# Unused matrix products tied to batch 0's transposed tiles, and another spacing of batch 1's Fourier steps

## The chip, the cores and the metric

The kernel runs on one core of one Trainium2 chip. The core has a matrix engine (TensorE, PE in the rows, with its weight loads as PEld), a vector engine (VectorE, DVE), a scalar engine (ScalarE, ACT), GpSimd (POOL) and a queue engine (SyncE, SP) that issues most transfers. The metric is the time of one execution in microseconds (us).

## The reference

For 8 batches of 576 positions, 8 heads of 64: attention with a window of 128 keys and a bias that falls with distance; the heads side by side are x (576 x 512). Then the real part of a Fourier transform over positions and features, added to x; a normalization per position; a two-layer net with ReLU, added again.

```python
attn = exp(scores - max) / (sum + 1e-09)        # |rel| bias, 0 <= rel < 128
x = (attn @ v).transpose(0, 2, 1, 3).reshape(B, S, 512)
u = x + real(fft(fft(x, axis=1), axis=2))
un = (u - mean(u)) / sqrt(var(u) + 1e-06)
out = u + relu(un @ w_ch1) @ w_ch2               # 512 -> 2048 -> 512
```

## The kernel before

Work is cut into batches and, in a batch, into four pairs of heads; p counts pairs over all batches (p = 4 b + j). One pair has three groups of scores (`scores`, L378); each group's result is reduced on DVE (L391, which also makes the row's minimum `nb`), put through the exponential on ACT and multiplied with v (`values`, into `pv`). Batches 0 and 1 (`NF = 2`) do this in fp32: the exponentials P are transposed on TensorE (`turn`, L422, into the PSUM tile `sp`), ACT copies them into an SBUF tile `pt` (L426, six buffers), and `values` multiplies `pt` with `vr` (L440). From batch 2 on all is split into fp16 high and low parts, and `pt` comes by a transposing DMA (L413).

After a batch's attention comes its Fourier transform (`fourier`): `fold_a` to `fold_d` (DVE, ACT), four `rows` (PE, L555), `middle`, three `cols` (PE, L589) with `cols_out` (ACT) and `cols_add` (DVE: `ds`, `X`, `ut`, L607 to L618), then `norm` (DVE, POOL, ACT `un`) and a transposing DMA into `uT`. Then the net (`ffn`): W1 products (L699) into `fp`, ACT's ReLU (L704) and DVE's remainder into `hbuf`, W2 products (L713) into `fp`. In the first 100 us the weights are read from DRAM as 64-bit words and put together by ACT (L183) and three DVE operations per chunk (L188 to L190), 32 chunks in all; four small products per chunk (`gram`, L198) find their scale.

The order of the work is set in two steps. Each piece is put into a queue with a due time (`put`, and `after`, which adds to the time of the piece at work); pieces are taken in order of due time, and this order is the priority with which a scheduler (with a model of the engines) then places every instruction in its engine's own order. On the chip each engine takes its instructions in just that order and waits where one isn't ready. `PACE`, `T1`, `DFT` and `START` set the due times of batches; in `fourier` the factor `f` spaces the transform's steps.

Some matrix products are computed and never read: `busy(p)` issues three of them (`SPIN`) after each `scores`, each `turn` and each `values` of batch 0's pairs (p < 4), of 128 x 512 columns, from the cosine table `tab1_sb` into a PSUM tile `spin`, an `fp` buffer. That is 15 calls for each of the four pairs, 180 products (L299).

Of the kernel before, what the change touches and what calls it, by code (L numbers as in the profile page):

```python
# [12 lines left out]
BF16 = mybir.dt.bfloat16  # L13
# [35 lines left out]
DFT = 24 + LC + 0.4  # L49
START = DFT + 17  # L50
PACE, T1 = (0.37, 0.5), 9.0
SPIN = 3
SLOW = 1.4


def begin_of(p):
    return 6 * PACE[0] * p if p < 4 else T1 + 6 * (p - 4)
# [19 lines left out]
def attn_fft_ffn_kernel(  # L77
# [16 lines left out]
    V, A, G, T = nc.vector, nc.scalar, nc.gpsimd, nc.tensor  # L94
# [14 lines left out]
    tab1_sb = const.tile([128, 4, 3, NS], F16, name="tab1_sb")  # L109
# [44 lines left out]
    def put(t, f, *a):  # L154
        heappush(queue, (t, next(order), f, a))

    def after(dt, f, *a, **kw):
        put(now[0] + dt, lambda: f(*a, **kw))  # L158
# [133 lines left out]

    raws, ops, Ps, pts, pvs, vmx = {}, {}, {}, {}, {}, {}
    spin = ps_f.tile([128, 512], F32, name="fp")
    trig = tab1_sb.rearrange("p a b c -> p (a b c)")

    def busy(p):
        for _ in range(SPIN if p < 4 else 0):
            T.matmul(spin, trig[:, 0:128], trig[:, 0:512], start=True, stop=True)  # L299

    def load(p):
        b, j = divmod(p, 4)
# [53 lines left out]
    def keys(t, ti):  # L356
        a0 = TILES[ti][2][0][1]
        if ti == 2:
            return view(t, 128, (65, 2), (1, 128))
        return t[:, a0:a0 + 128 * len(TILES[ti][2])]  # L360

    def scores(p, i):
        b, j = divmod(p, 4)
        if b < NF:
            prods = ((ops[p][0], ops[p][1]),)
        else:
            qh, ql, kh, kl = ops[p][:4]
            prods = ((qh, kh), (ql, kh), (qh, kl))
        grp = SGRP[i]
        sp = [ps_s.tile([128, 512], F32, name=f"sp{e}") for e in range(2)]  # L370
        col = 0
        for ti in grp:
            c0, m, blks = TILES[ti]
            n = 128 * len(blks)
            for x, (qq, kk) in enumerate(prods):
                for e in range(2):
                    h = slice(64 * e, 64 * e + 64)
                    T.matmul(sp[e][:m, col:col + n], qq[h, c0:c0 + m], keys(kk[h], ti),  # L378
                             start=(x == 0), stop=(x == len(prods) - 1))
            col += n  # L380
        busy(p)
        P = Ps[p, i] = {}
        for e in range(2):
            h = 2 * j + e
            nb = small.tile([128, 5], F32, name="nb", bufs=6)
            col = 0
            for ti in grp:
                m, n, pc = TILES[ti][1], 128 * len(TILES[ti][2]), PCOL[ti]
                pt = P[e, ti] = att.tile([128, 256], F32, name="P", bufs=PB)
                tab, mul = (rel_sb, -2.0 ** -(h + 1)) if b < NF else (scs[b][2], scs[b][1][:m, h:h + 1])  # L390
                V.tensor_tensor_reduce(pt[:m, 0:n], sp[e][:m, col:col + n], tab[:m, pc:pc + n],  # L391
                                       mul, 3.0e38, ALU.add, ALU.min, nb[:m, ti:ti + 1])
                after(0.25, A.activation, pt[:m, 0:n], pt[:m, 0:n], AF.Exp, bias=nb[:m, ti:ti + 1], scale=-1.0)
                if b >= NF:
                    after(0.45, halves, p, i, e, ti)
                col += n
# [18 lines left out]
    def turn(p, i, e):  # L415
        tp = ps_s.tile([128, 512], F32, name=f"sp{e}")
        P = Ps[p, i]
        col = 0
        for ti in TGRP[i]:
            m, blks = TILES[ti][1:]  # L420
            for x in range(len(blks)):
                T.transpose(tp[:, col:col + m], P[e, ti][:m, 128 * x:128 * x + 128], ident[:m, :m])  # L422
                col += m
        pt = pts[p, i, e] = att.tile([128, 448], F32, name="pt", bufs=6)
        busy(p)
        A.activation(pt[:, :col], tp[:, :col], AF.Copy)  # L426

    def values(p, i, e):
        b, j = divmod(p, 4)
        pt = pts.pop((p, i, e))  # L430
        if i == 0:
            pvs[p] = ps_v.tile([128, 512], F32, name="pv")[:, 0:325].rearrange("p (a b) -> p a b", a=5)
        pv, col = pvs[p], 0
        for ti in TGRP[i]:
            m, blks = TILES[ti][1:]
            n = len(blks)
            for x, (vc, _) in enumerate(blks):
                first, last = x == 0, x == n - 1
                if b < NF:
                    T.matmul(pv[:, ti], pt[:, col:col + 128], ops[p][2][:, e, vc], start=first, stop=last)  # L440
                    col += m
                    continue
                vh, vl = ops[p][4:]
                ph, pl = (pt[:, o:o + 128] for o in (POUT[ti] + x * m, POUT[ti] + (n + x) * m))
                T.matmul(pv[:, ti], ph, vh[:, e, vc], start=first, stop=False)  # L445
                T.matmul(pv[:, ti, 0:D], ph, vl[:, e, vc], start=False, stop=False)  # L446
                T.matmul(pv[:, ti], pl, vh[:, e, vc], start=False, stop=last)  # L447
        busy(p)
        if i == 2:
            after(0.2, weigh, p, e, pv)  # L450

# [42 lines left out]
    def fourier(b, t0):  # L494
# [122 lines left out]
                V.tensor_tensor(ut[p0:p0 + 32], X2[0:32], ds[0:32, 0:512], ALU.add)  # L617
                V.tensor_tensor(ut[p0 + 64:p0 + 96], X2[64:96], ds[64:96, 0:512], ALU.add)  # L618

        f = SLOW if b else PACE[1]  # L620
        put(t0, begin)
        for c, t in ((2, 0.0), (0, 0.8), (1, 1.5)):
            if c < 2:
# [99 lines left out]
    for p in range(4 * B):  # L723
        b, j = divmod(p, 4)
        t, f = begin_of(p), 1 if b else PACE[0]
        put(t - 7 * f if p else -3.2, load, p)
        if b < NF:
            put(t - 3.8 * f if p else -2, convert, p, 0)
            put(t - 1.2 * f, load_v, p)
            put(t + 4.2 * f, v_max, p)  # L730
        else:
            early = p < 4 * NF + 2
            put(t - (1.3 if early else 6.8), load_v, p)
            for what, x in enumerate((4.6, 3.6, -2 if early else 1.2)):
                put(t - x, convert, p, what)
        for i in range(3):
            put(t + 2 * i * f, scores, p, i)
            for e in range(2 if b < NF else 0):
                put(t + (2 * i + e + LB + 0.33) * f, turn, p, i, e)
        for x in range(6):  # L740
            put(t + (x + LC + 0.66) * f, values, p, x % 3, x // 3)
        if b < NF and j == 3:
            put(t + 5 * f, f32_scale, b)
# [5 lines left out]
    for b in range(B):  # L749
        t = begin_of(4 * b)  # L750
        if b >= NF:
            batch_scales(b, *((t - 16.4, 0.72) if b == NF else (t - 26, 1.2)))
        fourier(b, transform_of(b))
        n = 80 if b % 2 else 64
        t = forward_of(b)
        put(t, step, ffn(b), t, (24 if b else forward_of(1) - t) / n)
# [87 lines left out]
def program(q, k, v, moe_w_ch1, moe_w_ch2):  # L844
    import numpy as np
    import concourse.bacc as bacc

    B = q.shape[0]
    qa = np.ascontiguousarray(q.transpose(0, 1, 3, 2)[..., query_order()]).reshape(B, 4, 128, NQ)
    ka = np.concatenate([k, k[:, :, :NK - S]], axis=2).transpose(0, 1, 3, 2)  # L850
    ka = np.ascontiguousarray(ka).reshape(B, 4, 128, NK)
    idx = np.array([[min(s + p, S - 1) for s in VSTART] for p in range(128)])
    va = np.ascontiguousarray(v[:, :, idx])
    nf = min(B, NF)
    v0 = np.ones((nf, H, 128, 5, 65), np.float32)
    v0[..., 0:D] = va[:nf]
    w1 = np.ascontiguousarray(moe_w_ch1.reshape(4, 128, 16, 128).transpose(1, 2, 0, 3).reshape(128, -1))
    w2 = np.ascontiguousarray(moe_w_ch2.reshape(16, 128, DM).transpose(1, 0, 2).reshape(128, -1))
    w1, w2 = w1.view(np.int64), w2.view(np.int64)
    rel, slope, tab1, tab2 = tables()  # L860
    nc = bacc.Bacc("TRN2", target_bir_lowering=False, num_devices=1, dynamic_dma_scratch_size=1024)
    arrays, args = {}, []
    for name, a in (("q", qa), ("k", ka), ("v", va), ("v0", v0), ("w1", w1), ("w2", w2), ("rel", rel),
                    ("slope", slope), ("tab1", tab1), ("tab2", tab2)):
        arrays[name + "_dram"] = a
        args.append(nc.dram_tensor(name + "_dram", a.shape, mybir.dt.from_np(a.dtype), kind="ExternalInput").ap())
    rows = B * S
    args.append(nc.dram_tensor("out_dram", (rows, DM), F32, kind="ExternalOutput").ap())
    with tile.TileContext(nc, schedule_with_timeline_sim=True) as tc:
        attn_fft_ffn_kernel(tc, *args)  # L870
    return nc, arrays, B
```

## Time and profile before

| | us |
|---|---|
| median of 3 runs (lowest, highest) | 1116.77 (1116.02, 1118.63) |
| the profiled execution's own time | 1116.72 |
| its span, first to last instruction | 1114.9 |
| TensorE busy / VectorE busy / ScalarE busy | 1069.6 / 712.8 / 580.8 |
| mean granted TensorE clock | 0.972 of full speed |

[...] In a window's row, the number after x counts instructions.

### The profile page before, as it was taken

Reading aid. Unit: us, or ns where it says so; the run is one execution under the profiler, and the core shown is the slowest. Engines: PE = TensorE matmul, PEld = TensorE weight load, DVE = VectorE, ACT = ScalarE, POOL = GpSimd, SP = SyncE. Lnnn points to the kernel's source line nnn. Section 1 sums busy time; section 2 is a strip of 40 time slices with the busy share of each in tenths; the row PEclk is TensorE's granted clock in tenths of the full one; section 3 lists DMA queues with packets and bytes.
Section 4 is the critical chain, followed back from the end, with each engine's and each line's share of the span. In section 5 each row is a group of like instructions: output and inputs, shape, how many; then the busy total and the mean of one; then the engine's idle time right before and its main releaser. Section 6 shows DMA issues by size and latency. Waiting matters only on the chain.

```text
span 1114.9 us, 23952 instructions
## 1 busy us (share of the span) xinstructions
PE 1069.6 (96%) x9296; PEld 737.2 (66%) x9296; DVE 712.8 (64%) x2081; ACT 580.8 (52%) x1380; POOL 20.3 (2%) x59
## 2 busy tenths in 40 slices
PE   6999989879699999999999999999999999999998
PEld 4667768465374857767667677585758577767665
DVE  6988678815966667777868485869685655262111
ACT  5757889647863555446645464456635441151000
POOL 0000000000000000000000000000000000010000
PEclk9999859999899999999999999999999999999999
DMA  9941558656775235432642154344532240020000
GB/s 367 341 153 44 172 131 205 162 156 158 202 145 133 68 82 112 88 97 50 131 106 78 44 110 98 92 77 101 115 83 44 53 89 1 20 48 20 19 11 20
DMA packets 191507, 117.83 MB, mean 106 GB/s; under 512 B 154400, under 2 KB 164128, under 8 KB 191392
## 3 DMA queue, kind: packets, MB, share of 16 engines
q1 hardware_dynamic: 190816, 114.84, 40.8%
q8 instruction: 73, 1.20, 0.5%
q10 hardware_dynamic: 576, 1.45, 0.3%
q14 instruction: 42, 0.34, 0.1%
HBM read 70.63 MB, written 9.44 MB: 72 GB/s over the span
## 4 chain that ended last, share of the span: by engine, by line
PE 69%; DMA 7%; DVE 6%; ACT 3%; issue 1%; SPq 1%; ACTq 0%; DVEq 0%
PE fp L699 29%; PE fp L713 29%; PE sp L378 4%; PE pd L555 2%; DMA pt<-P 2%; DMA wall<-v_dram 2%; DMA wall<-q_dram 2%; ACT wall L257 1%; PE pd L589 1%; PE pv L445 1%; DMA wall<-k_dram 1%; PE pv L447 1%; PE pv L446 1%; DVE P L391 1%; DMA uT<-un 1%
## 5 line engine op out<-in xcount | busy, mean ns | idle before, releaser
L713 PE MATMUL fp<-wall,hbuf 128*128 128x512 f16 x1728 | 397.1, 383 | 2.4 <-DVE hbuf L158 2.3
L699 PEld LDWEIGHTS <-wall 128*128 128x128 f16 x3840 | 340.1, 99 | 61.3 <-issue 14.5
L699 PE MATMUL fp<-uT,wall 128*128 128x256 f16 x3072 | 364.8, 276 | 14.0 <-DVE hbuf L158 8.3
L713 PEld LDWEIGHTS <-hbuf 128*128 128x128 f16 x1728 | 163.2, 99 | 187.2 <-issue 11.5
L158 ACT ACTIVATE P<-P,nb 128x256 f32<-128x256 f32 x320 | 142.9, 479 | 124.6 <-DVE nb L391 124.5
L158 DVE SCALAR_TENSOR_TENSOR hbuf<-fp,hbuf 128x512 f16<-128x512 f32 x144 | 99.0, 688 | 130.4 <-ACT hbuf L704 130.0
L704 ACT ACTIVATE hbuf<-fp 128x512 f16<-128x512 f32 x144 | 85.1, 591 | 186.7 <-PE fp L699 186.5
L391 DVE CUSTOM_DVE_ANT_0 P<-sp,rg,nsl 128x256 f32<-128x256 f32 x240 | 97.3, 450 | 59.7 <-PE sp L378 51.9
L158 DVE SCALAR_TENSOR_TENSOR P<-P 128x256 f16<-128x256 f32 x240 | 88.6, 390 | 26.9 <-ACT P L404 25.6
L378 PE MATMUL sp<-kk,qq 64*128 64x256 f16 (+5 forms) x880 | 93.4, 294 | 11.5 <-DVE nb L391 5.9
L404 ACT ACTIVATE P<-P 128x256 f16<-128x256 f32 x240 | 86.0, 384 | 7.6 <-DMA pt<-P 7.0
L257 ACT ACTIVATE wall<-wall 128x512 f32<-128x512 f32 (+2 forms) x90 | 54.6, 606 | 49.5 <-DMA wall<-v_dram 19.2
L445 PE MATMUL pv<-vhs,pt 128*128 128x65 f16 x432 | 55.5, 195 | 4.6 <-DMA pt<-P 3.4
L446 PE MATMUL pv<-vl,pt 128*128 128x64 f16 x432 | 56.0, 193 | 0.0
L447 PE MATMUL pv<-vhs,pt 128*128 128x65 f16 x432 | 55.9, 194 | 0.0
L158 DVE SCALAR_TENSOR_TENSOR X<-fp,misc,X 128x512 f32<-128x512 f32 x32 | 23.8, 744 | 44.7 <-PE fp L713 44.7
L378 PEld LDWEIGHTS <-qq 64*128 64x128 f16 (+1 forms) x720 | 32.3, 100 | 28.5 <-issue 24.9
L445 PEld LDWEIGHTS <-pt 128*128 128x128 f16 x432 | 41.1, 98 | 15.0 <-issue 4.5
L299 PE MATMUL fp<-tab_sb 128*128 128x512 f16 x180 | 45.5, 379 | 1.1 <-DMA tab_sb<-tab_dram 1.1
L699 PE MATMUL fp<-wall,wall 128*128 128x128 f16 x768 | 45.4, 219 | 0.1
L446 PEld LDWEIGHTS <-pt 128*128 128x128 f16 x432 | 40.7, 99 | 7.0
L440 PE MATMUL pv<-vr,pt 128*128 128x65 f32 x288 | 41.3, 294 | 0.3 <-ACT pt L426 0.3
(146 smaller groups left out, 1200.4 us busy)
## 6 DMA issues: line engine op xcount, KB each, us to landing
qr<-q_dram SPq DMA_DIRECT2D x32, 304.0 KB, 3.1
hbuf<-w_dram SPq DMA_DIRECT2D x16, 512.0 KB, 7.2
out_dram<-X SPq DMA_DIRECT2D x32, 256.0 KB, 2.2
wall<-v_dram SPq DMA_DIRECT2D x30, 256.0 KB, 2.9
vr<-v_dram SPq DMA_DIRECT2D x24, 320.0 KB, 3.6
kr<-k_dram SPq DMA_DIRECT2D x24, 289.0 KB, 3.4
wall<-q_dram SPq DMA_DIRECT2D x24, 256.0 KB, 2.9
wall<-k_dram SPq DMA_DIRECT2D x24, 256.0 KB, 2.9
```

What stands on the lines that cost most here:

```text
L158: put(now[0] + dt, lambda: f(*a, **kw))
L257: A.activation(t, t, AF.Square, accum_out=box["mx"][:, i, c:c + 1])
L299: T.matmul(spin, trig[:, 0:128], trig[:, 0:512], start=True, stop=True)
L378: T.matmul(sp[e][:m, col:col + n], qq[h, c0:c0 + m], keys(kk[h], ti), start=(x == 0), stop=(x == len(prods) - 1))
L391: V.tensor_tensor_reduce(pt[:m, 0:n], sp[e][:m, col:col + n], tab[:m, pc:pc + n], mul, 3.0e38, ALU.add, ALU.min, nb[:m, ti:ti + 1])
L404: A.activation(hi, P32, AF.Copy, scale=2.0 ** 14)
L445: T.matmul(pv[:, ti], ph, vh[:, e, vc], start=first, stop=False)
L446: T.matmul(pv[:, ti, 0:D], ph, vl[:, e, vc], start=False, stop=False)
L447: T.matmul(pv[:, ti], pl, vh[:, e, vc], start=False, stop=last)
L699: T.matmul(fp[:, i * n:(i + 1) * n], w1_ap(e, c, f0 + i), uT[:, j, c, 0:n], start=(c == 0 and p == 0), stop=(c == 3 and p == 2))
L704: A.activation(ht[:, 0], fp, AF.Relu)
L713: T.matmul(op, hh[f][:, a, i * 128:(i + 1) * 128], w2_ap(e, f), start=(f == 0 and p == 0), stop=(f == 15 and p == 2))
```

## The change

`busy` and its calls go. `idle_turns(pt)` takes their place: after the copy of a transposed tile into `pt`, for the pairs of batch 0 alone, six products of 128 x 256 columns are queued with a due time 1.2 later than the piece at work. They read the upper halves of the words of that `pt` (as bfloat16) and write the same unused PSUM tile. There are six such copies per pair and four pairs: 144 products. In `fourier`, `f` is 0.9 for batch 1 where it was `SLOW` = 1.4; batch 0 keeps 0.5 and the later ones 1.4.

```diff
--- before.py
+++ after.py
@@ -49,7 +49,7 @@
 DFT = 24 + LC + 0.4
 START = DFT + 17
 PACE, T1 = (0.37, 0.5), 9.0
-SPIN = 3
+SPIN, GAP = 6, 1.2
 SLOW = 1.4
 
 
@@ -292,11 +292,11 @@
 
     raws, ops, Ps, pts, pvs, vmx = {}, {}, {}, {}, {}, {}
     spin = ps_f.tile([128, 512], F32, name="fp")
-    trig = tab1_sb.rearrange("p a b c -> p (a b c)")
-
-    def busy(p):
-        for _ in range(SPIN if p < 4 else 0):
-            T.matmul(spin, trig[:, 0:128], trig[:, 0:512], start=True, stop=True)
+
+    def idle_turns(pt):
+        upper = pt[:, 0:256].bitcast(BF16).rearrange("p (x e) -> p x e", e=2)[:, :, 1]
+        for _ in range(SPIN):
+            T.matmul(spin[:, 0:256], upper[:, 0:128], upper, start=True, stop=True)
 
     def load(p):
         b, j = divmod(p, 4)
@@ -378,7 +378,6 @@
                     T.matmul(sp[e][:m, col:col + n], qq[h, c0:c0 + m], keys(kk[h], ti),
                              start=(x == 0), stop=(x == len(prods) - 1))
             col += n
-        busy(p)
         P = Ps[p, i] = {}
         for e in range(2):
             h = 2 * j + e
@@ -422,8 +421,9 @@
                 T.transpose(tp[:, col:col + m], P[e, ti][:m, 128 * x:128 * x + 128], ident[:m, :m])
                 col += m
         pt = pts[p, i, e] = att.tile([128, 448], F32, name="pt", bufs=6)
-        busy(p)
         A.activation(pt[:, :col], tp[:, :col], AF.Copy)
+        if p < 4:
+            after(GAP, idle_turns, pt)
 
     def values(p, i, e):
         b, j = divmod(p, 4)
@@ -445,7 +445,6 @@
                 T.matmul(pv[:, ti], ph, vh[:, e, vc], start=first, stop=False)
                 T.matmul(pv[:, ti, 0:D], ph, vl[:, e, vc], start=False, stop=False)
                 T.matmul(pv[:, ti], pl, vh[:, e, vc], start=False, stop=last)
-        busy(p)
         if i == 2:
             after(0.2, weigh, p, e, pv)
 
@@ -617,7 +616,7 @@
                 V.tensor_tensor(ut[p0:p0 + 32], X2[0:32], ds[0:32, 0:512], ALU.add)
                 V.tensor_tensor(ut[p0 + 64:p0 + 96], X2[64:96], ds[64:96, 0:512], ALU.add)
 
-        f = SLOW if b else PACE[1]
+        f = (SLOW if b > 1 else 0.9) if b else PACE[1]
         put(t0, begin)
         for c, t in ((2, 0.0), (0, 0.8), (1, 1.5)):
             if c < 2:
```

The first place is TensorE's order at the start of the program (before; `tab_sb` is the cosine table, `wall` the weights under assembly, L422 the transposes):

```order
L378 MATMUL sp_162<-kk,qq 96x256
L378 MATMUL sp_163<-kk,qq 96x256
L299 LDWEIGHTS tab_sb
L299 MATMUL fp<-tab_sb 128x512
...
L198 LDWEIGHTS wall_105
L198 MATMUL fp<-wall_105 128x128
...
L422 MATMUL sp_183<-ident,P 128x128 x3
L422 MATMUL sp_205<-ident,P 128x128 x3
L378 MATMUL sp_218<-kk,qq 128x256
L378 MATMUL sp_219<-kk,qq 128x256
L299 LDWEIGHTS tab_sb
```

The same place now (line numbers from here on are one less for `turn`, L421):

```order
L378 MATMUL sp_159<-kk,qq 96x256
L378 MATMUL sp_160<-kk,qq 96x256
L198 LDWEIGHTS wall_105
L198 MATMUL fp<-wall_105 128x128
...
L421 MATMUL sp_177<-ident,P 128x128 x3
L421 MATMUL sp_196<-ident,P 128x128 x3
L378 MATMUL sp_206<-kk,qq 128x256
L378 MATMUL sp_207<-kk,qq 128x256
L421 MATMUL sp_220<-ident,P 128x96 x2
L421 MATMUL sp_220<-ident,P 128x128 x2
L299 LDWEIGHTS pt
L299 MATMUL fp<-pt 128x256
```

Twelve products stood between the first scores and the first `gram`; now none stands there, and the first six come after the third group of transposes, with `pt` as their operand.

The second place is VectorE's order at the end of batch 1's transform (before; `ds`, `X`, `ut` are its last `cols_add`, `st` and `ag` its norm, L391 the reductions of scores):

```order
L391 ISA P,nb<-sp_3554,rg,nsl 96x256
L391 ISA nb 96x1
L607 TENSOR_TENSOR ds<-ab 33x257
...
L614 TENSOR_TENSOR X<-X,ds 1x512
L617 TENSOR_TENSOR ut<-X,ds 32x512
L618 TENSOR_TENSOR ut<-X,ds 32x512
L158 TENSOR_TENSOR un<-un 128x512
L661 BN_STATS st<-X 128x6 x2
L158 SCALAR_TENSOR_TENSOR X<-fp,misc,X 128x512
...
L391 ISA P,nb<-sp_3661,rg,nsl 128x256
```

The same place now (`r<-pd` begins the scales of batch 3, without which its scores can't start):

```order
L390 ISA P,nb<-sp_3330,rg,nsl 128x256
L390 ISA nb 128x1
L665 SCALAR_TENSOR_TENSOR nmr<-ag,rstd 128x2
L606 TENSOR_TENSOR ds<-ab 33x257
...
L613 TENSOR_TENSOR X<-X,ds 1x512
L616 TENSOR_TENSOR ut<-X,ds 32x512
L158 SCALAR_TENSOR_TENSOR X<-fp,misc,X 128x512
L617 TENSOR_TENSOR ut<-X,ds 32x512
...
L660 BN_STATS st<-X 128x6 x2
L147 TENSOR_SCALAR r<-pd 128x3
```

The last `cols_add` of batch 1 was rows 632 to 638 of VectorE's order and is now rows 586 to 594; the `r` of batch 3 is row 597 before and row 598 now, so the transform's end has moved from behind it to ahead of it.

## Rows read from the trace of the kernel before

**Rows 1.** The page: span, busy times, TensorE clock in tenths over 40 slices.

```profile
span 1114.9 us, 23952 instructions
PE 1069.6 (96%) x9296; PEld 737.2 (66%) x9296; DVE 712.8 (64%) x2081; ACT 580.8 (52%) x1380; POOL 20.3 (2%) x59
...
PEclk9999859999899999999999999999999999999999
```

**Rows 2.** Windows, per stretch: length, busy us and (x count) per engine, clock, DMA.

```profile
core 0: us, PE busy (x) PEld busy (x) DVE busy (x) ACT busy (x) POOL busy (x), PEclk, DMA share, GB/s
10.00:110.00 100.00, 96.82 (x675) 64.55 (x676) 90.49 (x268) 71.12 (x145) 0.11 (x1) 1.00 0.63 221
350.00:1115.00 765.00, 759.81 (x6984) 522.78 (x6982) 462.13 (x1313) 329.60 (x770) 14.32 (x33) 1.00 0.31 69
```

**Rows 3.** Windows of three stretches of the startup, columns as in Rows 2.

```profile
10.00:30.00 20.00, 17.98 (x112) 10.65 (x112) 18.69 (x55) 15.42 (x35) 0.00 (x0) 1.00 1.03 402
30.00:60.00 30.00, 30.00 (x200) 18.70 (x197) 29.97 (x87) 22.30 (x45) 0.00 (x0) 1.00 0.88 308
60.00:110.00 50.00, 48.84 (x369) 35.19 (x369) 41.83 (x129) 33.41 (x66) 0.11 (x1) 1.00 0.31 97
```

**Rows 4.** Page, part 5: the unused products, and the 256-column products of fp16.

```profile
L699 PE MATMUL fp<-uT,wall 128*128 128x256 f16 x3072 | 364.8, 276 | 14.0 <-DVE hbuf L158 8.3
...
L299 PE MATMUL fp<-tab_sb 128*128 128x512 f16 x180 | 45.5, 379 | 1.1 <-DMA tab_sb<-tab_dram 1.1
```

**Rows 5.** Waits of DVE, 60 to 110 us: total us, times, longest.

```profile
DVE ri L459 <- PE pv L440: 2.7, 1, 2.7
DVE wall L219 <- ACT wall L216: 2.5, 4, 1.3
DVE P L391 <- PE sp L378: 1.6, 2, 1.1
```

**Rows 6.** Waits of PE, 100 to 345 us, same columns.

```profile
PE sp L378 <- DVE nb L391: 5.4, 3, 4.9
...
PE pv L440 <- ACT pt L426: 0.3, 1, 0.3
```

**Rows 7.** Windows around the change of level at 138 us, columns as in Rows 2.

```profile
132.00:138.00 6.00, 5.59 (x47) 4.14 (x44) 4.10 (x17) 5.95 (x20) 0.20 (x2) 1.00 0.59 188
138.00:166.00 28.00, 24.19 (x96) 18.34 (x97) 20.24 (x84) 23.23 (x52) 1.56 (x4) 0.51 0.48 128
```

**Rows 8.** Timeline of PE: products of values (L440), and the first of rows (L555).

```profile
79.88 2.12 PE L440 MATMUL pv<-vr,pt 128*128 128x65 f32 x18
...
109.24 0.30 PE L555 MATMUL fp<-tab_sb,fh 128*128 128x289 f16 x1 [0.86 <-ACT fh L538]
...
153.04 4.10 PE L440 MATMUL pv<-vr,pt 128*128 128x65 f32 x18
```

**Rows 9.** Timeline of DVE near 295 us: start, us, operation.

```profile
293.46 0.08 DVE L391 DVE_READ_ACCUMULATOR2_ANT nb<- 96x1 f32 x1
296.45 0.68 DVE L618 TENSOR_TENSOR ut<-X,ds 32x512 f32<-32x512 f32 x1
```

**Rows 10.** Windows of 10 us later on, columns as in Rows 2.

```profile
230.00:240.00 10.00, 8.47 (x72) 7.01 (x72) 2.44 (x4) 5.43 (x16) 0.00 (x0) 0.83 0.55 147
290.00:300.00 10.00, 6.12 (x66) 3.28 (x64) 9.63 (x24) 10.00 (x23) 0.00 (x0) 0.96 0.54 153
300.00:310.00 10.00, 7.05 (x41) 4.99 (x41) 8.00 (x28) 7.18 (x18) 1.77 (x2) 0.53 1.05 244
```

**Rows 11.** Timeline of PE: three runs of W1 products after 230 us.

```profile
231.53 4.16 PE L699 MATMUL fp<-uT,wall 128*128 128x256 f16 x24 [3.31 <-DVE hbuf L158]
...
305.04 7.56 PE L699 MATMUL fp<-uT,wall 128*128 128x256 f16 x48 [1.38 <-DMA uT<-un]
...
321.73 5.41 PE L699 MATMUL fp<-uT,wall 128*128 128x256 f16 x48
```


## The prediction

> **What bounds the kernel now.** I read the page first: TensorE is busy for 96% of the span at a clock of 9 tenths or more in most slices, VectorE and ScalarE for about half to two thirds [rows 1]. A share over the whole span hides stages, so the windows came next. From 350 us to the end TensorE is busy for 759.8 of 765 us at the full clock; from 10 to 110 us it is nearly so too, but there VectorE is busy for 90.5 of the 100 us [rows 2]. Then I cut the startup into three: from 10 to 30 us the DMA engines are full, from 30 to 60 us both TensorE (30.00 of 30) and VectorE (29.97) are, from 60 to 110 us TensorE alone is (48.84 of 50; VectorE 41.83, DMA share 0.31) [rows 3]. Between 110 and 350 us TensorE waits here and there and runs at the lower clock in stretches.
>
> So a microsecond taken from TensorE counts fully only after 350 us, where the change takes nothing: apart from names and numbers TensorE's order there is the one it was. It counts in part from 60 to 110 us, and hardly before that. Whatever the program gains by 350 us it keeps to the end, since TensorE has hardly any idle time left in which to lose it.
>
> **The change part by part.**
>
> *The unused products.* Before, 180 products take 45.5 us of busy TensorE, 45.5 / 180 = 253 ns each [rows 4], all in the startup. The 144 new ones have half the columns. No row shows one on `pt`; the nearest is the fp16 product of 256 columns, 364.8 / 3072 = 119 ns [rows 4], with its own weight load, as here. 144 x 0.119 = 17.1 us. TensorE is relieved of 45.5 - 17.1 = 28.4 us.
>
> What that is worth by 110 us is another matter. VectorE has nearly the same operations as before in that stretch (joining weights, reducing scores), and their 90.5 us [rows 2] fit into no less than 90.5 us: the relief can bring at most 9.5 us, of which 50 - 41.83 = 8.2 us lie after 60 us [rows 3]. The least is 0: then ScalarE, the transfers and VectorE itself set the pace. Between these I take what VectorE waited for TensorE by name from 60 to 110 us: 2.7 us for `values` and 1.6 us for `scores` [rows 5], 4.3 us. The third wait there, 2.5 us, is for ScalarE and stays. **Term 1: -4.3 us.**
>
> *The wait that this adds.* The first of each six products needs ScalarE's copy in `pt`. Behind it in TensorE's order stand the next transposes, scores or grams, and VectorE waits for those. Another reader of the same copies, `values`, waited for them once, 0.3 us, from 100 to 345 us [rows 6]. With 4 x 6 = 24 groups that bounds the cost between 0 and 7.2 us. I take 0, as the one wait of its kind is the nearest row and TensorE has 28.4 us to hide it in; without that cover it would be the 7.2 us. A copy isn't held longer either: the products are due 1.2 after it is made, `values` (LC + 0.66 - LB - 0.33) x 0.37 = 1.23 after it.
>
> *The clock.* [...] I price it at 0 in the sum: 17.1 us of dense products stay and are spread over the transposes. The other end is a rival below.
>
> [...]
>
> *Batch 1's transform.* With f = 0.9 its steps stand closer together. No instruction comes or goes; its last `cols_add` moves from row 632 to row 586 of VectorE's order, from behind the start of batch 3's scales to ahead of it. Before, that part ran from 293.5 us to 297.1 us on a VectorE that was busy for 9.63 of the 10 us around it [rows 9, 10], and TensorE's scores behind it waited for `nb`, 4.9 us at the longest [rows 6]. The first W1 products of batch 1 then waited 1.38 us for `uT` and took 7.56 us instead of the 5.41 us of an equal run at the upper level [rows 11], 2.15 us more, as the clock had fallen to 0.53 in that window [rows 10]. If all of it goes that is 4.9 + 1.4 + 2.2 = 8.5 us. The least is a loss: the 297.13 - 293.46 = 3.7 us of VectorE [rows 9] could fall ahead of a `hbuf` for which TensorE waits, as it did for 3.31 us at 228 us [rows 11]. The cover is that VectorE is busy for just 2.44 of 10 us there, ScalarE for 5.43 [rows 10]; without it the 3.7 us are paid. I take the longest wait alone, since the chain from `ut` over `un` and the transposing DMA to `uT` keeps its length. **Term 2: -4.9 us.** The five transposing DMAs of `uT` go past some fetches on SP's queue; their end was 1.38 us late [rows 11], so I count nothing for that and no more than 1.4 us. What is late next are the `hbuf` waits, which the change leaves.
>
> *The sum.* The profiled execution took 1116.72 us, 1.8 us more than its span of 1114.9 us [rows 1] and within 0.1 us of the median, 1116.77 us. 1116.72 - 4.3 - 4.9 = 1107.5 us.
>
> **The rivals.**
>
> *More comes of it.* VectorE closes all its gaps in the startup (9.5 us) and all three losses near 300 us go (8.5 us): 1116.7 - 18.0 = 1098.7 us. For it: TensorE is the only full engine after 60 us [rows 3]. Against it: VectorE also waits for ScalarE [rows 5], and engines that feed each other do not fill every gap.
>
> *Nothing comes of it.* The products were hidden behind VectorE and the DMA engines, full until 60 us [rows 3], and the wait for `nb` only changes its place, as the later scores of batch 3 still need batch 3's scales first: 1116.7 us. For it: 29.97 of 30 us [rows 3]. Against it: 4.3 us of waits on TensorE by name [rows 5].
>
> *The clock falls in the startup, and it is slower.* The place is 10 to 110 us. TensorE's work there is 96.8 - 45.5 + 17.1 = 68.4 us at the upper level; every two us at the lower level cost one, by 4.10 against 2.12 us [rows 8]. Up to 2 x (100 - 68.4) = 63 us at the lower level are thus covered, and with term 2, 2 x (100 - 68.4 + 4.9) = 73 us: from there on it decides. With 73 us the time is as before; with all 100 us it is 68.4 + 50 - 100 - 4.9 = 13.5 us more, 1130.2 us; I put the case at the middle, 1123.5 us. For it: what followed the products before [rows 7, 8]. Against it: the fall before came only after the last of the products, and here six still stand behind every transposed tile of batch 0. [...]
>
> **How the numbers follow.** The forecast, 1107.5 us with its own range of 1102 to 1113 us (each term by half of itself, and a little), has a chance of 0.50; more 0.16; nothing 0.14; the clock 0.20. Slower and faster cases both count, so the range reaches to them: 1095 us takes in the larger gain and some us beyond it; 1122 us takes in "nothing" and about half of the clock's case. About 0.1 stay outside on the upper side and less below. A measurement of this kernel can tell 0.2%, 2.2 us, from no change. Faster by more than that are the first two cases, 0.66; the same is 0.14; slower is 0.20.
>
> **What would show it.** Term 1 is right if the first `rows` product (109.24 us before [rows 8]) starts 3 to 6 us earlier with VectorE busier than 90.5% up to it; wrong if it starts no earlier, or with a clock clearly under 1.00 before it. The products' price is right at about 119 ns each, the added wait if no wait of L299 for `pt` adds up to more than 2 us. Term 2 is right if no wait of scores for `nb` near 4.9 us is left before batch 1's W1 products, and these start without a wait for `uT`. The steady part from 350 us on has to take the same time as before; if it doesn't, what I said of TensorE's order is wrong.

## The result, and the profile after

The changed kernel takes 1107.03 us (median of 4 runs, 1104.11 to 1108.68) against 1116.72 us before (4 runs, 1116.02 to 1118.63): a ratio of 0.9908, 95% interval 0.9883 to 0.9932. Run again later it took 1109.45 us (6 runs, 1106.63 to 1110.18) against 1115.78 us (29 runs), 0.9941 (0.9918 to 0.9964). All ratios leave out executions that took over 1.5% longer than the fastest of the same kernel; the medians are of all. The kernel before spread from 1109.2 to 1121.0 us over three such sessions, so in one profiled execution a stage differs by some us without a cause in the code; where one of the changed kernel is read below, its second profile mostly stands beside it. The profiled execution of the first session took 1104.11 us, the shortest of its four; the second profile, 1109.41 us, lies at its kernel's median.

The page after (span, busy times, TensorE's clock in tenths over 40 slices), which answers to [rows 1]:

```profile
span 1102.3 us, 23881 instructions
PE 1056.0 (96%) x9260; PEld 738.6 (67%) x9260; DVE 711.4 (65%) x2081; ACT 581.7 (53%) x1380; POOL 19.8 (2%) x59
...
PEclk8988869999899999999999999999999999999999
```

"Busy" is time in which an engine had an instruction at work. The clock is a share of full speed; in the profiles before and after, it stands at 1.00 or at 0.50 (before: 1.00 from 119 to 138 us, 0.50 from 139 to 166 us), called the full or upper and the lower level here.

Span less busy is TensorE's idle time: 1102.3 - 1056.0 = 46.3 us, before 1114.9 - 1069.6 = 45.3 us. The 12.6 us of span came out of busy TensorE time, not out of waiting: the unused products take 45.5 - 23.0 = 22.5 us less, and 8.9 us of that came back in other work, by my estimate some 3.5 us of it at the lower level, which lasts for about 68 us in all where it was 61 us; 18 products of `values` took 4.10 us in it against 2.12 us [rows 8]. The windows, which answer to [rows 2, 3] (length, busy us and count per engine, granted clock, DMA):

```profile
10.00:110.00 100.00, 91.61 (x665) 71.82 (x665) 93.72 (x294) 73.86 (x155) 0.43 (x2) 0.88 0.66 228
10.00:30.00 20.00, 17.60 (x104) 12.89 (x105) 17.61 (x59) 15.01 (x35) 0.00 (x0) 0.74 1.03 403
30.00:60.00 30.00, 28.93 (x250) 23.82 (x249) 29.97 (x91) 24.53 (x54) 0.00 (x0) 1.00 0.89 304
60.00:110.00 50.00, 45.08 (x315) 35.11 (x313) 46.14 (x146) 34.32 (x68) 0.43 (x2) 0.87 0.37 112
350.00:1102.00 752.00, 744.89 (x6856) 512.88 (x6854) 454.19 (x1290) 328.45 (x772) 14.12 (x32) 1.00 0.31 71
```

In the startup TensorE is down from 96.82 to 91.61 us and VectorE up from 90.49 to 93.72 us; from 60 to 110 us VectorE, 41.83 us before, is now the busier of the two. But the clock from 10 to 110 us, 1.00 before, is now 0.88 (0.92 in the second profile). TensorE's first `rows` product and its unused products (page, part 5: count, busy us, mean ns, idle us ahead):

```profile
103.43 0.30 PE L554 MATMUL fp<-tab_sb,fh 128*128 128x289 f16 x1
```

```profile
L299 PE MATMUL fp<-pt 128*128 128x256 bf16 x144 | 23.0, 296 | 0.0
```

The `rows` product starts 109.24 - 103.43 = 5.8 us earlier [rows 8]; in the second profile it starts at 104.0 us, 5.2 us earlier. The 144 products take 160 ns each, not 119 [rows 4]. By stretches of 10 us (their busy time, then the clock):

```profile
10.00:20.00 10.00, 2.16 (x10) 1.50 (x11) 0.58 1.04 402
...
30.00:40.00 10.00, 4.09 (x30) 2.65 (x28) 1.00 0.80 262
40.00:50.00 10.00, 3.56 (x24) 2.12 (x24) 1.00 0.93 326
50.00:60.00 10.00, 2.09 (x14) 1.23 (x14) 1.00 0.93 325
60.00:70.00 10.00, 1.12 (x7) 0.82 (x8) 0.81 0.60 200
70.00:80.00 10.00, 5.37 (x33) 3.11 (x32) 0.85 0.67 201
```

In the three stretches at 1.00 that is 9.74 us for 68, 143 ns; in the one at 0.58 it is 2.16 us for 10, 216 ns. They run from 17 to 84 us, among the work that they follow.

Later on, TensorE's waits from 255 to 370 us (us in total, times, longest), after:

```profile
PE fp L698 <- DVE hbuf L158: 5.4, 2, 3.7
PE fp L698 <- DMA uT<-un: 2.2, 1, 2.2
PE fp L712 <- DVE hbuf L158: 2.1, 1, 2.1
PE pd L588 <- ACT ab L600: 1.6, 1, 1.6
PE pv L445 <- DMA wall<-k_dram: 1.4, 1, 1.4
```

The wait for `nb`, 4.9 us [rows 6], is gone. That for `uT` isn't: 1.38 us before [rows 11], now 2.16 us, and a `hbuf` wait of 3.7 us stands behind it:

```profile
284.63 0.61 PE L698 MATMUL fp<-uT,wall 128*128 128x256 f16 x2 [2.16 <-DMA uT<-un]
...
297.69 3.06 PE L698 MATMUL fp<-uT,wall 128*128 128x256 f16 x16 [3.66 <-DVE hbuf L158]
```

The windows of the kernel before and of the kernel after, from 300 to 350 us (PE busy is the number after the length, the clock stands ahead of the DMA share):

```profile
300.00:350.00 50.00, 42.83 (x336) 30.41 (x336) 36.13 (x109) 34.27 (x84) 1.79 (x3) 0.87 0.74 171
```

```profile
300.00:350.00 50.00, 47.88 (x390) 31.75 (x389) 34.88 (x101) 29.04 (x74) 0.10 (x1) 0.95 0.69 175
```

5.1 us more of busy TensorE at a higher clock. Counted back along TensorE's timeline, the last 6500 products stand in the same order in all kernels of this document. They start at 388.5 us, before at 401.5 us: the kernel after leads by 401.5 - 388.5 = 13.0 us there, and at the end by 12.6 us, so from there on it gains nothing more. In the second profile they start at 393.1 us, a lead of 8.4 us, with 7.3 us at the end.

### The profile page after: what moved, and what is told of

The parts are those of the page before. It is cut to its first block, busy times and chain, and to the rows that moved or that the text cites. A ratio compares the mean times of both kernels' runs of the same rounds, so it can differ in the third digit from the quotient of the medians.

```text
span 1102.3 us, 23881 instructions
## 1 busy us (share of the span) xinstructions
PE 1056.0 (96%) x9260; PEld 738.6 (67%) x9260; DVE 711.4 (65%) x2081; ACT 581.7 (53%) x1380; POOL 19.8 (2%) x59
## 4 chain that ended last, share of the span: by engine, by line
PE 71%; DMA 10%; DVE 9%; ACT 6%; issue 2%; SPq 1%; ACTq 0%; DVEq 0%
PE fp L698 28%; PE fp L712 27%; PE sp L378 5%; PE pd L554 3%; DMA wall<-q_dram 2%; ACT wall L257 2%; DMA wall<-k_dram 2%; DMA wall<-v_dram 2%; PE pv L440 1%; ACT P L158 1%; PE pd L588 1%; DVE P L390 1%; PE pv L445 1%; DMA pt<-P 1%; DVE wall L190 1%
## 5 line engine op out<-in xcount | busy, mean ns | idle before, releaser
L712 PE MATMUL fp<-wall,hbuf 128*128 128x512 f16 x1728 | 393.0, 381 | 2.1 <-DVE hbuf L158 2.1
L698 PEld LDWEIGHTS <-wall 128*128 128x128 f16 x3840 | 339.8, 99 | 61.8 <-issue 13.3
L440 PE MATMUL pv<-vr,pt 128*128 128x65 f32 x288 | 43.2, 305 | 0.9 <-DVE X L462 0.8
L440 PEld LDWEIGHTS pv<-vr,pt 128*128 128x128 f32 x288 | 40.9, 222 | 3.8 <-DVE X L462 1.4
```

The lines of the kernel that those rows point to most:

```text
L698: T.matmul(fp[:, i * n:(i + 1) * n], w1_ap(e, c, f0 + i), uT[:, j, c, 0:n], start=(c == 0 and p == 0), stop=(c == 3 and p == 2))
L712: T.matmul(op, hh[f][:, a, i * 128:(i + 1) * 128], w2_ap(e, f), start=(f == 0 and p == 0), stop=(f == 15 and p == 2))
```

## The experiments

My theory was the prediction's: less TensorE work in the startup brings about 4 us, the steps bring about 5 us, and the clock costs nothing as long as enough work is off TensorE. The rivals: the clock holds the startup, and what counts is how many products there are and where; and the steps alone, or the products alone, bring it all. Each kernel was timed beside the kernel before (1115.10, 1115.78 and 1116.58 us in the three sessions). The unused products feed no output in any of them. In the table the ratio has its 95% interval; "rows" is the start of the first `rows` product, "low" the time at the lower level between 60 and 110 us, "tail" the start of the last 6500 products, all three of one profiled execution, in us.

| kernel | us | ratio | rows | low | tail |
|---|---|---|---|---|---|
| before | | 1 | 109.2 | 0 | 401.5 |
| changed, first / again | 1107.03 / 1109.45 | 0.9908 / 0.9941 | 103.4 / 104.0 | 13.1 / 15.3 | 388.5 / 393.1 |
| products alone | 1112.74 | 0.9981 (0.9965-0.9998) | 103.0 | 13.7 | 395.3 |
| steps alone | 1113.17 | 0.9979 (0.9958-0.9999) | 109.5 | 0 | 402.3 |
| no products, steps | 1122.85 | 1.0023 (0.9993-1.0053) | 103.8 | 19.3 | 395.7 |
| half width, old places | 1108.95 | 0.9942 (0.9922-0.9962) | 108.4 | 25.7 | 394.3 |
| half width and steps | 1111.89 | 0.9967 (0.9950-0.9984) | 114.8 | 40.4 | 398.8 |
| 144 from the table | 1120.15 | 1.0038 (1.0018-1.0058) | 109.2 | 37.5 | 404.0 |
| 12 per tile | 1114.88 | 0.9988 (0.9972-1.0004) | 108.9 | 0 | 401.3 |
| 3 per tile | 1130.84 | 1.0109 (1.0072-1.0146) | 112.4 | 13.6 | 416.3 |
| batch 1 too | 1116.80 | 1.0002 (0.9984-1.0020) | 103.1 | 6.8 | 399.3 |
| f = 0.7 | 1109.51 | 0.9933 (0.9909-0.9957) | 103.8 | 15.3 | 394.0 |
| f = 1.15 | 1115.83 | 0.9997 (0.9979-1.0014) | 103.1 | 13.3 | 397.6 |

From "tail" to the end all fourteen profiled executions take 712 to 716 us. What tells these executions apart has thus happened before.

**The two parts apart.** Products alone is the changed kernel with the old steps (the diff); steps alone is the kernel before with the new ones (the same line the other way round).

```diff
-        f = (SLOW if b > 1 else 0.9) if b else PACE[1]
+        f = SLOW if b else PACE[1]
```

> The changed kernel with f = 1.4 again for batch 1: only the unused products are changed. Theory (two terms that add up): the products alone give what the first Fourier product showed, 4 to 6 us, so 1111 to 1113 us, with the first rows product about 6 us earlier than before and the end of batch 1's transform as late as before. Rival (the products give all): 1107 us. Rival (the steps give all): 1117 us.

> The kernel before with f = 0.9 for batch 1: only the steps are changed, the 180 products of 512 columns stay. Theory (two terms): 4 to 6 us less than before, 1111 to 1113 us, the first rows product where it was (109 us), and no wait of 4.9 us of scores for nb near 300 us. Rival (the products give all): 1117 us. Rival (the steps give all): 1107 us.

Each part alone brings some 2 us, less than the 4 to 6 us expected of either, and both intervals end just short of 1: -2.4 us and -1.9 us, together -4.3 us where the whole change brought -9.7 and -6.3 us. Their product, 0.9960, lies outside the first interval of the changed kernel and inside the second, so that they bring more together is likely and not shown. The products alone give the whole of the startup's gain: `rows` starts at 103.0 us, 6.2 us earlier, and the tail also 6.2 us earlier; the time gains less. The waits of TensorE from 255 to 370 us, products alone:

```profile
PE pv L445 <- DMA pt<-P: 4.3, 3, 2.7
PE pv L445 <- DVE X L462: 3.8, 2, 3.6
PE pd L570 <- DVE zl L563: 2.7, 1, 2.7
PE sp L378 <- DVE nb L390: 1.9, 2, 1.0
```

And with the steps alone:

```profile
PE pv L445 <- DVE nsl L275: 3.9, 1, 3.9
PE pv L445 <- DVE X L463: 2.3, 1, 2.3
PE fp L699 <- DMA uT<-un: 1.8, 1, 1.8
```

The long wait for `nb` is gone in both, with the old `f` as well as with the new one. With the products alone batch 1's last `ut` starts at 294.8 us, still behind batch 3's `r` at 280.5 us, so that wait goes without the move ahead of batch 3's scales; with the steps alone the `ut` is ahead (290.9 against 291.6 us), and the tail is no earlier than before (402.3 us, in an execution of 1116.36 us, above the median of its kernel). With the steps alone one for `nsl`, 3.9 us, has come in its place: there the rival that the wait only changes its place is right.

**No products at all.** SPIN = 0 with the new steps.

```diff
-SPIN, GAP = 6, 1.2
+SPIN, GAP = 0, 1.2
```

> The changed kernel with no unused products at all (SPIN = 0). Theory: VectorE and the transfers already bound the startup, so the 17 us of TensorE work that go bring nothing, and the clock falls a little more often: 1106 to 1112 us. Rival (the products hold the clock, and the startup hangs on it): the startup at the lower level for most of its length, the first rows product later than 109 us, 1117 us or more. Rival (TensorE still bounds the startup): another 4 us or more less, 1103 us or below.

My theory failed in the time. The median is 1122.85 us, over a spread of 1112.16 to 1133.52 us; by its ratio, 1.0023, this kernel is as fast as the one before, where the changed one stands at 0.9908 and 0.9941. The profiled execution was the fastest of the twelve, with two windows:

```profile
10.00:60.00 50.00, 41.81 (x250) 32.20 (x250) 48.50 (x147) 38.72 (x85) 0.00 (x0) 0.82 0.96 349
60.00:110.00 50.00, 48.34 (x296) 38.07 (x296) 47.14 (x153) 37.99 (x78) 0.21 (x2) 0.81 0.36 107
```

The products are worth their time. That they are so by holding the clock in the startup, as the rival said, this trace does not show: the level is low for 37.7 of the 100 us from 10 us on (23.3 and 15.2 us in the changed kernel's two profiles), but the `rows` product starts at 103.8 us, as early as there. Over the twelve executions a lower mean clock goes with a longer time (0.955 to 0.968 in the five up to 1116 us, 0.945 to 0.951 in the seven above 1122 us), which fits the rival; in which stage the longer ones lose it is open.

**Half width at the old places.** The kernel before, its 180 products of half the columns; and the same with the new steps.

```diff
-            T.matmul(spin, trig[:, 0:128], trig[:, 0:512], start=True, stop=True)
+            T.matmul(spin[:, 0:256], trig[:, 0:128], trig[:, 0:256], start=True, stop=True)
```

> The kernel before with its 180 products at the same places in the program, but of 256 columns: only the columns are taken away. 180 x 0.119 = 21 us of products stay of 45.5. Theory (what counts is TensorE's work): 4 to 6 us less than before, 1111 to 1113 us, as with the products tied to pt. Rival (what counts is the low priority and the place behind pt): 1116 to 1118 us.

> The kernel before with products of 256 columns and f = 0.9 for batch 1. Theory (TensorE's relief and the steps are what counts, not the tie to pt): as the changed kernel within 3 us, 5 to 10 us under before. Rival (tie and low priority count by themselves): no better than the half width alone, 6 us under before or less, and 4 us or more over the changed kernel.

Half width alone, 1108.95 us, is better than the theory's 1111 to 1113 us and as good as the second run of the changed kernel, without any tie to `pt`. Its `rows` product is hardly earlier, by 0.9 us, but its tail is, by 7.2 us: the gain is made in between, and which part of the new order makes it is not shown. The products have all ended by 60 us, and the level falls at 84 us:

```profile
60.00:84.00 24.00, 21.94 (x187) 17.33 (x184) 23.62 (x85) 17.87 (x40) 0.11 (x1) 1.00 0.46 137
84.00:115.00 31.00, 29.36 (x105) 21.55 (x106) 24.69 (x70) 22.48 (x46) 0.10 (x1) 0.50 0.37 107
```

The steps added nothing to it: 1111.89 us is within the theory's 3 us of the changed kernel, but only 3.9 us under before. Each such edit lets the scheduler order everything up to some 385 us anew, and here the lower level lasts from 69.6 to 120.8 us.

**The tie to `pt`.** The changed kernel, its products reading the cosine table; TensorE's timeline shows no idle time ahead of any of them.

```diff
-        upper = pt[:, 0:256].bitcast(BF16).rearrange("p (x e) -> p x e", e=2)[:, :, 1]
+        upper = tab1_sb.rearrange("p a b c -> p (a b c)")[:, 0:256]
```

> The changed kernel, its 144 products at the same low priority, but read from the cosine table instead of pt: no wait for the copies. Theory (the wait for pt costs nothing): within 3 us of the changed kernel. Rival (tying them to pt costs or spreads them): 5 us or more from it, faster if the wait costs, slower if the scheduler then bunches the products and the clock falls more in the startup.

The same number of products of the same size, and 1120.15 us. They crowd together (the products alone, busy us and count):

```profile
10.00:20.00 10.00, 5.42 (x36) 3.85 (x37) 1.00 1.03 401
20.00:30.00 10.00, 4.94 (x40) 3.67 (x38) 1.00 1.03 405
30.00:40.00 10.00, 4.61 (x37) 3.27 (x35) 1.00 0.94 325
40.00:50.00 10.00, 4.65 (x37) 3.40 (x36) 1.00 0.98 363
50.00:60.00 10.00, 0.00 (x0) 0.00 (x0) 1.00 0.91 320
60.00:70.00 10.00, 0.00 (x0) 0.00 (x0) 0.66 0.55 149
```

All are over by 50 us, and from 60 to 110 us TensorE, with none of them, is nearly full at a clock of 0.62:

```profile
60.00:110.00 50.00, 47.87 (x229) 37.22 (x229) 44.15 (x136) 35.04 (x68) 0.11 (x1) 0.62 0.34 97
```

The changed kernel took 1109.45 us in the same session, so at this low priority the tie to `pt` is worth 10.7 us, as the rival with the crowded products had it. The edit changes the operand too, to dense fp16; their price, 19.62 / 144 = 136 ns, is not what makes the difference.

**Their number.** Twelve per tile in place of six, and in a second kernel, edited in the same way, three.

```diff
-SPIN, GAP = 6, 1.2
+SPIN, GAP = 12, 1.2
```

> The changed kernel with 12 products behind each transposed tile of batch 0 instead of 6 (34 us of TensorE instead of 17). Theory (6 are near the best: fewer let the clock fall, more load a full TensorE): the clock stays at 1.00 up to 100 us, the first rows product 2 to 5 us later than with 6, and the time 1110 to 1114 us, between the changed kernel and before. Rival (the clock is what counts): faster than the changed kernel by 2 us or more.

> The changed kernel with 3 products behind each transposed tile of batch 0 (9 us of TensorE). Theory (the products hold the clock, none at all gave 1112 to 1134 us): between none and six, 1110 to 1118 us, with a wider spread over runs than the changed kernel's 4 us. Rival (TensorE's load still counts and three suffice for the clock): 1104 to 1107 us.

With twelve, at 1114.88 us, TensorE is where it was before, full at the full clock, and the gain is all but gone, as the theory had it (its range ended at 1114 us):

```profile
60.00:110.00 50.00, 49.36 (x423) 40.09 (x421) 43.90 (x133) 32.72 (x65) 0.11 (x1) 1.00 0.36 110
```

With three it is the slowest kernel of all, 1130.84 us, worse than I expected. The level is low from 34 to 44 us; from 30 to 60 us VectorE is busy for 27.70 us (after: 29.97 us), and it waits 6.8 us for scores up to 112 us (after: 3.4 us up to 104 us). Why its median is above that with none I can't say: the order differs too, and the two spreads overlap (1122.17 to 1141.63 us here).

**Batch 1 as well.** After each of batch 1's copies too, six products into the tile whose copy was just made, to hold the clock between 103 and 162 us.

```diff
-    def idle_turns(pt):
+    def idle_turns(pt, dst=spin):
...
-            T.matmul(spin[:, 0:256], upper[:, 0:128], upper, start=True, stop=True)
+            T.matmul(dst[:, 0:256], upper[:, 0:128], upper, start=True, stop=True)
...
+        else:
+            idle_turns(pt, tp)
```

> The changed kernel with six more products behind each transposed tile of batch 1 as well (144 more, 17 us of TensorE, into the PSUM tile just copied). Theory (the clock at its lower level from 103 to 121 and 141 to 162 us is what makes batch 1's attention late): these stretches shrink by half or more, the net of batch 0 starts 4 to 8 us earlier, the time falls to 1098 to 1103 us. Rival (ScalarE and VectorE bound that stretch, 10.0 and 9.2 of 10 us busy from 140 us): the clock stays up and the time is the changed kernel's within 3 us, or up to 6 us more for the added products.

The clock held, the time did not follow. The kernel after, and then with batch 1's products, 110 to 160 us:

```profile
110.00:160.00 50.00, 45.84 (x286) 35.93 (x285) 33.76 (x123) 42.40 (x110) 1.77 (x6) 0.70 0.54 135
```

```profile
110.00:160.00 50.00, 47.28 (x371) 37.28 (x370) 34.68 (x130) 44.57 (x114) 1.75 (x6) 0.93 0.52 139
```

By my estimate the clock's rise is worth (0.93 - 0.70) x 50 = 11.5 us of TensorE there, and the added products took 10.6 us in the same window: by these numbers they cost about what they bring. W1 starts at 155.3 us (after: 156.3). Then TensorE waits 7.4 us for `hbuf` at 227 us, and longest of all at 364 us (after: 3.7 us for `hbuf` at 298 us):

```profile
363.68 4.27 PE L700 MATMUL fp<-uT,wall 128*128 128x256 f16 x24 [9.67 <-DVE hbuf L158]
```

The order is new again, and of the startup's 6.1 us the tail keeps 2.2. At 1116.80 us, 7.4 us above the changed kernel in the same session, it is outside the rival's bound too.

**Other spacings, and the same kernel again.** `f` for batch 1 at 0.7, as shown, and at 1.15, in place of 0.9.

```diff
-        f = (SLOW if b > 1 else 0.9) if b else PACE[1]
+        f = (SLOW if b > 1 else 0.7) if b else PACE[1]
```

> The changed kernel with f = 0.7 for batch 1. Theory (the end of batch 1's transform has only to stand ahead of batch 3's scales; here rows 589 to 590 against 591, in the changed kernel 592 to 594 against 598): within 3 us of the changed kernel, 1106 to 1112 us. Rival (each step earlier is worth something more): 3 us or more below it. Rival (steps this close collide with the net of batch 0): 4 us or more above it.

> The changed kernel with f = 1.15 for batch 1, half way to the 1.4 of before. Theory (the place against batch 3's scales decides; here its end is rows 603 to 610, around their 606): between the products alone and the changed kernel, 1107 to 1113 us. Rival (only the steps' sum with the new startup order, by chance, made the changed kernel's second gain): no regular dependence on f, over 1113 us or under 1106 us.

> The changed kernel again, next to the others on one chip. Theory (the two parts add up, as 2.4 and 1.9 us measured apart): 4 to 5 us less than before, ratio 0.996. Rival (the two parts are worth more together than apart, since the steps let the startup's gain through the first stretch of batch 1's net): 8 to 11 us less, ratio 0.990 to 0.993.

0.7 is as good as 0.9. 1.15 lies between 0.9 and 1.4, but its time, 1115.83 us, is above both that of 0.9 and that of 1.4 (the products alone, 1112.74 us). This is the rival with no regular dependence on `f`: the steps' gain hangs on the order that comes out. The startup's gain is there (103.1 us) and is lost in part from 255 to 370 us, where TensorE waits, longest last:

```profile
PE pv L445 <- DMA pt<-P: 7.1, 2, 3.6
PE pv L445 <- DVE nmr L665: 5.1, 1, 5.1
PE pd L588 <- ACT ab L600: 2.8, 1, 2.8
PE fp L698 <- DMA uT<-un: 2.6, 1, 2.6
```

The changed kernel again gained 6.3 us, between the theory's 4 to 5 and the rival's 8 to 11. No kernel here beats it; f = 0.7 and half width equal its second run within their intervals.

## Why the prediction was right, and where not

The forecast was 1107.5 us; 1107.03 and 1109.45 us were measured. The sum came out, but not by its terms one by one, and in part by luck. In the second session, with 29 executions of the kernel before beside it, the gain was 6.3 us of the 9.2 forecast.

**From 110 us to the end.** The sum carries what the startup gains straight to the end. The runs do not bear that out between 110 and 400 us. Batch 1's products and f = 1.15 start `rows` at 103.1 us and take 1116.80 and 1115.83 us; half width starts it at 108.4 us and takes 1108.95 us. In the changed kernel the lead over before grew from 5.8 us at `rows` to 13.0 us at the tail (from 5.2 to 8.4 us in the second profile); with batch 1's products it shrank from 6.1 to 2.2 us. This stretch can make or lose as much as the startup, by waits that are other ones in each order; for it the sum had Term 2 alone.

**Term 1 (-4.3 us)** was about right in size, but not by its source. `rows` came 5.8 and 5.2 us earlier, 6.2 us with the products alone, inside the 3 to 6 us named, but for that last one; up to it, from 10 us on, VectorE is busy for 93% of the time in both profiles. The upper bound of [rows 2], 9.5 us, was not reached. VectorE's waits from 60 to 110 us, which answer to [rows 5], after and then in the second profile:

```profile
DVE P L390 <- PE sp L378: 2.2, 3, 0.8
DVE wall L188 <- ACT wall L183: 1.1, 1, 1.1
DVE ri L458 <- PE pv L440: 0.3, 1, 0.3
```

```profile
DVE P L390 <- PE sp L378: 4.4, 4, 2.2
DVE ri L458 <- PE pv L440: 0.5, 2, 0.3
```

The wait for `values`, 2.7 us, is nearly gone; that for scores grew from 1.6 to 2.2 and 4.4 us. So of the 4.3 us of waits on TensorE that I took for the gain, 2.5 and 4.9 us are there again. What went in both is the wait of `wall` L219 for ScalarE, 2.5 us, of which I had said that it stays. From 60 us to `rows` VectorE lost 4.3 us of idle time and 1.5 us of work that now stands elsewhere (2.9 and 2.3 us in the second profile).

**The products' price** was wrong: 160 ns, 143 at the full clock, not 119. The relief was 45.5 - 23.0 = 22.5 us, not 28.4; Term 1 was taken from the waits, so the sum did not use it.

**The added wait** was right at 0: no wait of the products for `pt` stands in the trace. The idle time ahead of their line, above, is 0.0; ahead of their weight loads it is 5.0 us, of which a release by ScalarE ended 0.4 us.

**The clock, put at 0,** was the step that failed in its reason. It fell, to 0.88, and I had called Term 1 wrong if it did. The 0 was an estimate: no run shows what sets the level, and what the two profiles show is 0.88 and 0.92 from 10 to 110 us, with `rows` 5.8 and 5.2 us earlier. That the gain came all the same fits the slower rival, by which lost clock is covered up to a point. That point I had worked out over 100 us at once, 63 us at the lower level. The runs speak for counting it by stage. Part of the table's "low" lies behind the start of `rows`, in the changed kernel 6.3 of 13.1 us. From 60 us up to `rows`, where TensorE was the full engine [rows 3], the kernels with six products a tile of `pt`, or none, are at the lower level for 6.8 to 13.1 us and start `rows` at 103.0 to 104.0 us; the half width and the crowded products, with 24.1 to 45.2 us of it, start it at 108.4 to 114.8 us; those with none of it, but TensorE full of products, at 108.9 to 109.5 us. Three per tile (13.6 us, 112.4 us) falls outside this; its loss begins before 60 us. The rival that I gave 0.20 is seen in the crowded products: 37.0 us low up to `rows`, which comes no earlier than before, and 1120.15 us. Thinned products are slower too (1130.84 us), and none at all bring nothing (ratio 1.0023), but their traces do not show that the startup's clock is why. The changed kernel stays clear of the rival with six products behind each tile. From 60 to 110 us the clock was 1.00 with twelve per tile (TensorE busy for 49.36 of 50 us) and 0.62 with the crowded products, which are over by 50 us (busy for 47.87 us). With half width it was 0.50 over 31 us of which TensorE was busy for 29.36 us, so the engine's busy time alone does not tell which level it had.

**Term 2 (-4.9 us)** is the least certain. The wait for `nb` went, as forecast; `uT` did not come in time, against the forecast (2.16 us, and 2.3 us in the second profile), and a `hbuf` wait of 3.7 us (3.8 us in the second) took a place that I had priced only as a bound. Steps alone are worth 1.9 us; added to the products they raised the gain from 2.4 to 6.3 and 9.7 us, by 3.9 to 7.3 us; added to half width, nothing. And with f = 1.15 the whole change is worth 0.8 us. What the steps bring thus depends on the order that the scheduler makes of the rest. That moving the last `cols_add` ahead of batch 3's scales is the cause is not shown: the long `nb` wait is also gone with the products alone, where that `cols_add` still stands behind them.

**The steady part** was right: from the start of the last 6500 products to the end 1102.3 - 388.5 = 713.8 us after, 714.5 us in the second profile, 713.5 us before.

What stays open: whether the two parts add up or help each other, what in the order from 110 to 400 us makes the rest of the gain, and why three products per tile are worse than none.

## What to carry to other kernels

Products that are never read cost time here where TensorE was full (twelve per tile: busy for 49.36 of 50 us from 60 to 110 us, 1114.88 us), and taking all of them away did not pay (1122.85 us): six per tile (1109.45 us) were better than three (1130.84 us), twelve or none. If such work gets a low priority, tie it to results that appear as the stage goes on, so that a scheduler can't run it all at the start (1120.15 against 1109.45 us here); half the width at the old places did as well (1108.95 us). An earlier end of one stage is not yet a gain: follow the lead on to the point from which all orders are the same. Where a scheduler plans everything anew after an edit, measure the parts together as well as apart.

## What the hardware showed that I had not expected

- One kernel's level differs between executions: the changed kernel was at the lower level from 11.6 to 21.8 us and from 103.7 to 120.8 us in one profile, in the other not at all before 64.0 us, and from 105.0 to 135.7 us; spans 1102.3 and 1107.6 us.
- With no unused products at all the same program took 1112.16 to 1133.52 us over twelve executions; with twelve per tile 1113.08 to 1119.73 us over twelve, with six 1106.63 to 1110.18 us over six. Three per tile did not steady it: 1122.17 to 1141.63 us over six.
- A bfloat16 product of 256 columns that reads every second half word of `pt` took 143 ns at the full clock among fp32 work, against 119 ns for the fp16 one of the net in its long runs. The dense fp16 products from the cosine table took 136 ns at the full clock among the same kind of work, so 17 of the 24 ns are there without the half words; where they come from is not shown.
